# Reordering k scalings on GpSimd, one pair of steps on TensorE at the start, and moving two last copies to VectorE in a fused linear-attention and MLP kernel

## Chip, cores, metric

One core of a Trainium2 chip. The metric is the device time of one execution in microseconds (us). In the profiles PE is TensorE, PEld its weight loads, DVE is VectorE, ACT is ScalarE, POOL is GpSimd, SP is SyncE; L170 is line 170 of the kernel. The tiles live in SBUF or, where TensorE writes, in banks of PSUM. An expert matmul is one of `x @ w_in` of the MLP (`h_ps`).

## The reference, cut

```python
# q, k, v: (4, 8, 768, 64) float32; lam: one decay per head
for b in range(nb):                                   # blocks of the sequence
    intra = (qb @ kb.T) * Dmask                       # scores, masked by powers of lam
    inter = (qb * lam_pow) @ kv_state
    out[block] = intra @ vb + inter
    kv_state = lam_block * kv_state + (kb * rev_pow).T @ vb
x = out.transpose(0, 2, 1, 3).reshape(3072, 512)
y = gelu_exact(x @ w_in) @ w_out                      # 512 -> 2048 -> 512
```

## The kernel before

It works on 24 chunks of 128 tokens (4 batches, 6 steps), and on the MLP in 6 groups of 4 chunks. The program gives every engine its order, and GpSimd's timeline of before shows it kept: q_hat of chunk 9 at 53.29, the four k_dec from 54.29, the next load issue at 58.27, as in the code below. Chunks 0 to 7 are transposed on TensorE, the others by DMA, after GpSimd has scaled q. The parts that matter here, cut:

```python
def decay_k(c, eng):                     # k times powers of lam, both operands in SBUF
    c.k_dec = work_pool.tile([128, H, D], BF16, tag="kd", name="k_dec", bufs=8)
    eng.tensor_mul(c.k_dec, c.k, lam_m[...])

def scores(c):                           # takes two PSUM banks of tag "sc" (4 banks in turn)
    sc_ps = [bank([128, HP, C], F32, "sc", f"sc_ps{hi}") for hi in range(2)]
    ...
    # VectorE: sc_m = sc_ps * dmask

def next_state(c):                       # one bank of the same tag "sc"
    kv_ps = bank([128, HP, 128], F32, "sc", "kv_ps")
    ...                                  # TensorE: kv_ps = k_dec.T @ v
    nc.vector.tensor_add(tmp, kv_ps, states[c.b])   # the sum: empties the bank
    nc.vector.tensor_mul(new, tmp, lam_blk)         # the product: both inputs in SBUF

def first_requests():                    # on GpSimd, all in this order
    for n in (8, 9):
        request(n)                       # q_hat = q * lam_p, then DMA transposes
    for n in range(4, 8):
        decay_k(live[n], nc.gpsimd)
    prefetch(11)                         # six load issues for chunks 10 and 11
    for n in (8, 9):
        decay_k(live[n], nc.gpsimd)
# on TensorE: kv(4, 5) before block (1, 6), kv(6, 7) before (1, 8), scores of 8 and 9 before (1, 12)
```

(2 * M is written as 8 here, and so on.) The four states of chunks 4 to 7 take the four "sc" banks just before the scores of chunks 8 and 9 take them again: the second bank of chunk 9's scores is the bank that the state of chunk 7 used.

## Time and profile before

| | before |
|---|---|
| median of the first 3 runs | 212.79 us (212.71 to 213.16) |
| span of the profile | 211.0 us |
| PE busy | 97% of the span |
| PE's wait for k_dec in this profile | 0.24 us |

TensorE is busy all through, so only its few waits count, and what follows its last matmul. The lines that show this are in the prediction. One more line of the timeline of VectorE before will be needed: the state products (L219), of which the first began 20 ns after GpSimd had begun a k_dec (57.29).

```profile
57.31 1.57 DVE L219 TENSOR_TENSOR state<-tmp,lam_blk 128x512 bf16<-128x512 f32 x1
59.52 0.69 DVE L219 TENSOR_TENSOR state<-tmp,lam_blk 128x512 bf16<-128x512 f32 x1
60.84 0.89 DVE L219 TENSOR_TENSOR state<-tmp,lam_blk 128x512 bf16<-128x512 f32 x1
62.37 0.81 DVE L219 TENSOR_TENSOR state<-tmp,lam_blk 128x512 bf16<-128x512 f32 x1
```

The columns are start, duration, engine, line, operation, tiles, shapes, number of instructions merged into the line; in brackets the idle time before it and what ended it.

### The profile page before, as it was taken

Reading aid. Unit: us, or ns where it says so; the run is one execution under the profiler, and the core shown is the slowest. Engines: PE = TensorE matmul, PEld = TensorE weight load, DVE = VectorE, ACT = ScalarE, POOL = GpSimd, SP = SyncE. Lnnn points to the kernel's source line nnn. Section 1 sums busy time; section 2 is a strip of 40 time slices with the busy share of each in tenths; the row PEclk is TensorE's granted clock in tenths of the full one; section 3 lists DMA queues with packets and bytes.
Section 4 is the critical chain, followed back from the end, with each engine's and each line's share of the span. In section 5 each row is a group of like instructions: output and inputs, shape, how many; then the busy total and the mean of one; then the engine's idle time right before and its main releaser. Section 6 shows DMA issues by size and latency. Waiting matters only on the chain.

```text
span 211.0 us, 3635 instructions
## 1 busy us (share of the span) xinstructions
PE 205.7 (97%) x1503; PEld 107.2 (51%) x1503; DVE 78.1 (37%) x124; ACT 86.6 (41%) x153; POOL 104.3 (49%) x119
## 2 busy tenths in 40 slices
PE   7999999999999999999999999999999999999994
PEld 2455574556664465444465444555444464444442
DVE  4783610175594136840414842244542240000000
ACT  5675662326556111556111556311465311566121
POOL 7994633883898964948978695940000000000000
PEclk9999999999999999999999999999999999999999
DMA  7999999999899699996999999996100012100112
GB/s 85 141 152 183 196 207 194 155 212 159 172 96 129 77 138 111 116 134 160 136 156 141 159 172 140 132 170 164 50 0 3 0 50 102 50 0 0 50 53 99
DMA packets 101328, 24.49 MB, mean 116 GB/s; under 512 B 92992, under 2 KB 98368, under 8 KB 101312
## 3 DMA queue, kind: packets, MB, share of 16 engines
q0 software_dynamic: 79120, 13.51, 84.3%
q1 hardware_dynamic: 22192, 10.76, 25.1%
q8 instruction: 12, 0.20, 0.4%
q14 instruction: 4, 0.03, 0.0%
HBM read 27.27 MB, written 6.29 MB: 159 GB/s over the span
## 4 chain that ended last, share of the span: by engine, by line
PE 71%; DMA 19%; POOL 8%; issue 1%; ACT 0%; POOLq 0%
PE o_ps L277 31%; PE h_ps L265 31%; DMA w_out_t<-in_moe_w_out_dram 7%; DMA w_in_t<-in_moe_w_in_dram 4%; DMA v_t<-in_v_dram 4%; DMA q_t<-in_q_dram 3%; PE sc_ps L199 2%; PE o_ps L232 2%; POOL k_dec L170 2%; PE o_ps L226 2%; PE o_ps L291 2%; POOL q_t L66 2%; PE kv_ps L211 1%; POOL k_t L66 1%; POOL v_t L66 1%
## 5 line engine op out<-in xcount | busy, mean ns | idle before, releaser
L265 PE MATMUL h_ps<-x_t,w_in_t 128*128 128x512 bf16 (+2 forms) x464 | 86.6, 343 | 0.1
L277 PE MATMUL o_ps<-w_out_t,g_t 128*128 128x512 bf16 x368 | 82.9, 379 | 0.0
L267 ACT ACTIVATE g_t<-h_ps 128x512 bf16<-128x512 f32 (+1 forms) x101 | 58.2, 576 | 33.9 <-PE h_ps L265 33.7
L265 PEld LDWEIGHTS <-w_in_t 128*128 128x128 bf16 x464 | 41.0, 98 | 39.9 <-DMA w_in_t<-in_moe_w_in_dram 0.2
L277 PEld LDWEIGHTS <-g_t 128*128 128x128 bf16 x368 | 35.0, 98 | 40.8
L203 DVE TENSOR_TENSOR sc_m<-sc_ps,dmask 128x512 bf16<-128x512 f32 x48 | 30.0, 682 | 39.2 <-PE sc_ps L199 39.2
L282 ACT COPY o_sb<-o_ps 128x512 f32<-128x512 f32 x23 | 13.5, 586 | 73.5 <-PE o_ps L277 73.5
L191 POOL TENSOR_TENSOR q_hat<-q_t,lam_p 128x512 bf16<-128x512 bf16 x16 | 17.0, 1065 | 23.2 <-DMA q_t<-in_q_dram 14.0
L66 POOL DMA_DIRECT2D q_t<-in_q_dram x24 | 21.6, 902 | 5.0 <-DMA w_out_t<-in_moe_w_out_dram 3.3
L66 POOL DMA_DIRECT2D k_t<-in_k_dram x24 | 22.1, 920 | 3.2 <-DMA w_out_t<-in_moe_w_out_dram 1.1
L66 POOL DMA_DIRECT2D v_t<-in_v_dram x23 | 20.9, 911 | 2.9 <-DMA w_out_t<-in_moe_w_out_dram 2.3
L238 DVE CAST x_t<-o_ps 128x512 bf16<-128x512 f32 x18 | 11.3, 684 | 19.8 <-PE o_ps L232 19.8
L170 POOL TENSOR_TENSOR k_dec<-k_t,lam_m 128x512 bf16<-128x512 bf16 x16 | 17.2, 1104 | 0.0
L218 DVE TENSOR_TENSOR tmp<-kv_ps,state 128x512 f32<-128x512 f32 x16 | 10.9, 683 | 10.1 <-PE kv_ps L211 10.1
L219 DVE TENSOR_TENSOR state<-tmp,lam_blk 128x512 bf16<-128x512 f32 x16 | 12.8, 803 | 0.5
L326 PE MATMUL idle_ps<-idle 128*128 128x512 bf16 x31 | 10.9, 477 | 1.2 <-DVE idle L106 1.2
L184 DVE TENSOR_TENSOR qT<-t_ps,lam_q 128x512 bf16<-128x512 bf16 x8 | 5.5, 688 | 14.1 <-PE t_ps L178 13.3
L199 PE MATMUL sc_ps<-qT,kT 64*128 64x128 bf16 x192 | 8.0, 217 | 0.9 <-DVE qT L184 0.6
L199 PEld LDWEIGHTS <-kT 64*128 64x128 bf16 x192 | 5.7, 94 | 5.8 <-issue 4.3
L232 PE MATMUL o_ps<-sc_m,v_t 128*64 128x128 bf16 x192 | 7.8, 222 | 0.0
L183 ACT COPY kT<-t_ps 128x512 bf16<-128x512 bf16 x8 | 4.7, 586 | 6.0 <-PE t_ps L178 5.8
L232 PEld LDWEIGHTS <-v_t 128*64 128x64 bf16 x192 | 5.8, 109 | 2.6 <-issue 0.7
(41 smaller groups left out, 71.9 us busy)
## 6 DMA issues: line engine op xcount, KB each, us to landing
out_dram<-o_sb SPq DMA_DIRECT2D x23, 256.0 KB, 2.4
k_t<-in_k_dram POOLq DMA_DIRECT2D x24, 128.0 KB, 4.9
q_t<-in_q_dram POOLq DMA_DIRECT2D x24, 128.0 KB, 5.4
v_t<-in_v_dram POOLq DMA_DIRECT2D x23, 128.0 KB, 5.9
w_out_t<-in_moe_w_out_dram POOLq DMA_DIRECT2D x4, 512.0 KB, 13.3
w_in_t<-in_moe_w_in_dram POOLq DMA_DIRECT2D x4, 384.0 KB, 9.8
w_in_t<-in_moe_w_in_dram POOLq DMA_DIRECT2D x2, 256.0 KB, 7.6
v_f<-in_v_dram SPq DMA_DIRECT2D x1, 256.0 KB, 3.5
```

What stands on the lines that cost most here:

```text
L66: nc.gpsimd.dma_start(raw[n, name], chunk_of(name, n))
L170: eng.tensor_mul(c.k_dec, c.k, lam_m[:, :, None].to_broadcast((128, H, D)))
L191: nc.gpsimd.tensor_mul(q_hat, c.q, lam_p[:, :, None].to_broadcast((128, H, D)))
L199: nc.tensor.matmul(sc_ps[hi][:, hp, :], c.kT[p, hp, :], c.qT[p, hp, :], start=True, stop=True)
L203: nc.vector.tensor_mul(c.sc_m[:, :, hi, :], sc_ps[hi], dmask_r[:, :, hi, :])
L219: nc.vector.tensor_mul(new, tmp, lam_blk)
L232: nc.tensor.matmul(c.o_ps[hi * D:(hi + 1) * D, hp, :], c.v[:, 2 * hp + hi, :], c.sc_m[:, hp, hi, :], start=(c.so == 0 and hp == 0), stop=T ...
L238: nc.vector.tensor_copy(x_o, c.o_ps)
L265: nc.tensor.matmul(h_ps[:, f, :], w, x_t[:, ki, lo:hi], start=(ki == 0 and f == 0), stop=(ki == NK1 - 1), skip_group_check=True)
L267: nc.scalar.activation(g_t[:, kf:kf + n_kf, lo:hi], h_ps, ACT.Gelu)
L277: nc.tensor.matmul(om[io], g_t[:, kf, io * C:(io + 1) * C], w_out_t[:, kf, :], start=(kf == 0), stop=(kf == NK2 - 1))
L282: nc.scalar.copy(o_sb, om[io])
```

## The change

The intent, part by part: GpSimd does the k_dec of chunks 4 to 7 while it would otherwise wait for q, so that the states don't wait; the scores of chunk 2 don't stand behind the outputs of chunk 1; the last rows leave PSUM through VectorE.

```diff
@@ mm2_cols
-                nc.scalar.copy(o_sb, o2)
+                nc.vector.tensor_copy(o_sb, o2)
@@ start
-    keep_warm(2)
+    keep_warm(4)
+    scores(live[2])
     outputs(live[1])
-    scores(live[2])
-    keep_warm(5)
+    keep_warm(4)
     outputs(live[2])
@@ first_requests
         for n in (2 * M, 2 * M + 1):
+            for m in (2 * n - 3 * M, 2 * n - 3 * M + 1):
+                decay_k(live[m], nc.gpsimd)
             request(n)
-        for n in range(M, 2 * M):
-            decay_k(live[n], nc.gpsimd)
         prefetch(2 * M + 3)
```

## The prediction

Where a cut is marked, figures and rules of the hardware are taken out that no trace or run shows. The sum keeps its terms, 0.24 + 0.05 + 0 = 0.29 us less and 0.05 back, 212.55; but what the end's 0 was worked out from, the cost of a copy on VectorE, is cut, so this 0 was the author's estimate and is not shown. Three things to know for reading: the 265 and 478 ns on ScalarE are the copies of 128 and 384 columns; the 0.85 for four idle matmuls is an estimate (in the profile of before the four from 14.98 start 0.215 to 0.227 us apart, and take 0.87 up to the next matmul); and that VectorE stands up to 1.0 us (rival A) is an estimate from the 1.57 us of the one product beside a k_dec and the 1.04 us of a k_dec.

> **What bounds the kernel now.** I read the page first (busy shares, the slices), then the waits, then the chain that ended last, and then the timelines of single engines around the three places that the diff touches: the start (11 to 16 us), the stretch where chunks 4 to 7 enter the state (48 to 63 us), and the end. The page says that TensorE is the bound nearly everywhere:
>
> ```profile
> PE 205.7 (97%) x1503; PEld 107.2 (51%) x1503; DVE 78.1 (37%) x124; ACT 86.6 (41%) x153; POOL 104.3 (49%) x119
> PE   7999999999999999999999999999999999999994
> PEclk9999999999999999999999999999999999999999
> ```
>
> PE is at nine tenths or more in 38 of 40 slices and the clock is granted throughout. Only what makes PE wait, or what follows its last matmul, can be won. The waits of the whole execution that hold up PE after the start are one line, and it belongs to the group that the diff moves (the weight loads of the state update waiting for GpSimd's scaled k):
>
> ```profile
> PE sc_ps L199 <- DVE qT L184: 0.6, 2, 0.4
> PEld L232 <- DMA v_t<-in_v_dram: 0.5, 1, 0.5
> PEld L211 <- POOL k_dec L170: 0.2, 1, 0.2
> ```
>
> The chain shows the same place: GpSimd, queued since the start behind its DMA issues and two scalings of q, releases the state matmuls at 58.39, and from there to the end everything is PE:
>
> ```profile
> 53.29 1.04 POOL q_hat L191
> 54.33 1.63 POOL k_dec L170 x2
> ...
> 56.29 2.05 POOL k_dec L170 x2
> 58.34 0.05 issue
> 58.39 0.40 PE kv_ps L211 x4
> ```
>
> GpSimd's 8% and the DMA's 19% in that chain are therefore not a prize of 27%: PE had other work meanwhile. The prize is PE's own stop. In PE's timeline the four state updates of that stretch come in two pairs:
>
> ```profile
> 56.16 0.62 PE L211 MATMUL kv_ps<-v_t,k_dec 128*128 128x128 bf16 x8
> 57.92 0.86 PE L211 MATMUL kv_ps<-v_t,k_dec 128*128 128x128 bf16 x8
> ```
>
> Same work, 0.62 against 0.86: the second pair stops 0.24 us in its middle, for k of chunk 7.
>
> [...] the product of tmp and lam_blk (both in SBUF) took 1.57 us at 57.31, beside GpSimd's k_dec, and 0.69 us at 59.52 beside DMA issues. The score masks and casts take one operand from PSUM and stay at 0.68 to 0.69. [...] The trace has ScalarE at 265 ns and 478 ns, and VectorE at 680 ns for 512 elements[...]. [...] The trace has a PE gap of 0.42 us at 8.16 with the clock at 1.00 afterwards[...].
>
> **The change, part by part.**
>
> **GpSimd's order.** Removed from behind q_hat 9: four k_dec (54.29 to 58.27, 3.98 us, 0.995 each from start to start). Added: k 4 and 5 ahead of q_hat 8, k 6 and 7 between q_hat 8 and q_hat 9. GpSimd's timeline has idle time just there:
>
> ```profile
> 47.24 0.88 POOL L66 DMA_DIRECT2D v_t<-in_v_dram  x1
> 50.91 1.04 POOL L191 TENSOR_TENSOR q_hat<-q_t,lam_p 128x512 bf16<-128x512 bf16 x1 [2.79 <-DMA q_t<-in_q_dram]
> 53.29 1.04 POOL L191 TENSOR_TENSOR q_hat<-q_t,lam_p 128x512 bf16<-128x512 bf16 x1 [1.34 <-DMA q_t<-in_q_dram]
> 54.29 4.04 POOL L170 TENSOR_TENSOR k_dec<-k_t,lam_m 128x512 bf16<-128x512 bf16 x4
> 58.27 0.94 POOL L66 DMA_DIRECT2D k_t<-in_k_dram  x1
> ```
>
> The gaps are 2.79 and 1.34 us. k of chunks 4 to 7 is on the chip (chunk 7's transpose runs at 49.2 on PE). So: k 4, 5 from 48.1 to 50.1, inside the gap of 2.79; q_hat 8 stays at 50.9; k 6, 7 from 51.9 to 53.9; q_hat 9 from 53.9 to 54.9, that is 0.6 later than 53.29; the next loads from 54.9 in place of 58.27, 3.3 us earlier (3.98 less 0.6). All four k_dec are done 2.2 us ahead of PE's 56.16, where before the last two ended at 57.3 and 58.3. PE's stop of 0.24 us goes, and nothing else on PE does: after 60 us its timeline has no wait left. The 3.3 us that GpSimd gains later are off the path.
>
> **The start.** One more idle matmul in all (4+4 for 2+5[...]) and the scores of chunk 2 ahead of the outputs of chunk 1. PE now:
>
> ```profile
> 11.55 0.59 PE L326 MATMUL idle_ps<-idle 128*128 128x512 bf16 x2
> 12.11 0.58 PE L232 MATMUL o_ps<-sc_m,v_t 128*64 128x128 bf16 x8
> 12.90 0.40 PE L199 MATMUL sc_ps<-qT,kT 64*128 64x128 bf16 x8 [0.21 <-DVE qT L184]
> 13.23 1.25 PE L326 MATMUL idle_ps<-idle 128*128 128x512 bf16 x5
> 14.42 0.63 PE L232 MATMUL o_ps<-sc_m,v_t 128*64 128x128 bf16 x8
> 14.98 1.04 PE L326 MATMUL idle_ps<-idle 128*128 128x512 bf16 x4
> 15.85 1.46 PE L265 MATMUL h_ps<-x_t,w_in_t 128*128 128x384 bf16 x8
> ```
>
> The scores of chunk 2 already wait for VectorE's qT, which runs 12.17 to 12.85 straight behind the masks of chunk 1. VectorE's order is not touched, so they start at 12.90 in either kernel. With the change four idle matmuls end at 11.55 + 0.85 = 12.40, PE waits half a microsecond, the scores run to 13.23, the outputs of chunk 1 take about 0.35, four idle matmuls 0.85 and a switch 0.1: outputs of chunk 2 from 14.53 in place of 14.42. But their second matmul needs the second mask, which VectorE ends at 14.61. It starts at 14.66 before, and can do so after. The last four idle matmuls and the first expert matmul at 15.85 stay. Sum: 0. A small gain is possible in executions where v of chunk 1 lands later than here (the wait of 0.5 above), because it then no longer holds the scores; I put 0.05 on it.
>
> **The end.** The last two evacuations move from ScalarE to VectorE. The one of 384 columns (0.48 us[...]) lies beside the last 16 matmuls. The one of 128 is on the path:
>
> ```profile
> 207.00 0.48 ACT L295 COPY o_sb<-o_ps 128x384 f32<-128x384 f32 x1 [1.97 <-PE o_ps L291]
> 207.50 1.01 SPq L296 DMA_DIRECT2D out_dram<-o_sb  x2
> 207.89 0.27 ACT L295 COPY o_sb<-o_ps 128x128 f32<-128x128 f32 x1 [0.42 <-PE o_ps L291]
> ```
>
> [...] VectorE starts perhaps 20 ns sooner after a matmul (13.32 after one that ends at 13.31; ScalarE 207.89 after 207.85). [...]
>
> **Sum**: 0.24 (state) + 0.05 (start) + 0 (end) = 0.29 us less, and 0.05 back for the risk in rival A, so 212.79 - 0.24 = 212.55.
>
> **The rivals.** A: a VectorE wait in place of the GpSimd wait. GpSimd now reaches k_dec of chunks 8 and 9 at 54.9 + 5.3 (six issues, 58.27 to 63.57) = 60.2. VectorE then does the state products of chunks 6 and 7, whose inputs are both in SBUF. By today's durations (0.72 and 0.61 from start to start) the product of chunk 6 starts at 59.97. If k_dec comes first, VectorE stands up to 1.0 us, the sum of chunk 7 ends near 62.5 in place of 62.33, and the scores of chunk 9, which take over that PSUM bank at about 62.0, wait 0.3 us: the gain is gone, 212.8. For it: the 1.57 us above. Against it: the first product is relieved of just that 0.9, so that VectorE is ahead by it, and 59.97 is before 60.2. One in four. B: q_hat 9 is 0.6 us later, and the loads of chunks 10 and 11 now run beside its DMA transposition, whose landing takes 2.4 to 6.0 us in this trace. Even at 6.0 it lands near 61.0, and its scores come at 62.0: 1 us in hand. If it doesn't hold, some tenths are lost: 212.9. One in fifteen. C: the whole GpSimd lead is worth more, because later loads and transpositions come 3.3 us earlier. Against it: no wait of PE after 60 us. It would take the time below 212.2; one in fifteen. D: the start is set by PE's order, not by VectorE's, and the extra idle matmul costs its 0.2, or the earlier scores win as much. Either moves the time by 0.2; one in six.
>
> **Range and chances.** The three runs before spread from 212.71 to 213.16, which is as much as the effect. Centre 212.55, with 0.4 down (C, or both small gains) and 0.4 up (A or B with a run at the upper edge): 212.15 to 212.95. 2% is 4.26 us, and the sum of PE's waits after the start is 0.24, so a change of 2% would take something that no view shows: 0.01 for either side, 0.98 for within.
>
> **What would show it.** In the changed kernel: no PE wait on k_dec, and both pairs of state matmuls at 0.62; GpSimd's loads after q_hat 9 near 54.9; scores of chunk 2 still near 12.9 from the span's start, ended by VectorE's qT, and the first expert matmul near 15.85; 16 score matmuls near 62.0 without a wait (with one: rival A, and a state product of over 1 us on VectorE before it)[...]. I am wrong if the first expert matmul moves by over 0.15 us, if the last copy takes over 0.35, or if a new wait shows at the scores of chunks 8 and 9.

## The result

Changed: 212.75 us median of 6 runs (212.16 to 213.04); before: 212.78 us median of 6 (212.56 to 213.16). The ratio is 0.9994, 95% interval 0.9979 to 1.001. The time is the same, though the wait that was to go is gone. PE's timeline of the changed kernel:

```profile
55.93 0.61 PE L211 MATMUL kv_ps<-v_t,k_dec 128*128 128x128 bf16 x8
...
57.68 0.61 PE L211 MATMUL kv_ps<-v_t,k_dec 128*128 128x128 bf16 x8
58.12 3.68 PE L265 MATMUL h_ps<-x_t,w_in_t 128*128 128x128 bf16 x39
61.73 0.97 PE L199 MATMUL sc_ps<-qT,kT 64*128 64x128 bf16 x16
62.64 3.63 PE L265 MATMUL h_ps<-x_t,w_in_t 128*128 128x512 bf16 x16
```

(This trace lacks some matmul records, 1480 on PE against 1504 weight loads, so counts such as x39 are one short.) Both pairs of state matmuls now take 0.61 us, where the second took 0.86. But the 16 score matmuls take 0.97 where they took 0.62. Before:

```profile
62.23 0.62 PE L199 MATMUL sc_ps<-qT,kT 64*128 64x128 bf16 x16
```

From the first state matmul to the first expert matmul behind the scores, which I call the stretch, it is 6.71 us (55.93 to 62.64) against 6.62 before (56.16 to 62.79; 6.63 from these rounded times). The chain of what ended last, changed kernel, shows who is in between (columns: start, duration, what):

```profile
57.08 1.10 DVE state L219
58.17 0.61 DVE tmp L218
58.79 0.02 issue
58.81 0.81 DVE state L219
59.62 0.61 DVE tmp L218
60.24 0.02 issue
60.26 1.41 DVE state L219
61.67 0.61 DVE tmp L218
62.28 0.04 issue
62.33 0.38 PE sc_ps L199 x7
```

In the chain of before, GpSimd's k_dec stood at this place and the scores ran through. Now VectorE's sums and products do: the sum of chunk 7 (61.67) ends at 62.28, and 0.05 later TensorE goes on with the last seven of chunk 9's eight score matmuls, the first of which writes the bank that that sum has emptied. GpSimd's timeline, changed kernel:

```profile
48.09 2.05 POOL L170 TENSOR_TENSOR k_dec<-k_t,lam_m 128x512 bf16<-128x512 bf16 x2
50.74 1.04 POOL L191 TENSOR_TENSOR q_hat<-q_t,lam_p 128x512 bf16<-128x512 bf16 x1 [0.60 <-ACT x_t L236]
51.74 2.04 POOL L170 TENSOR_TENSOR k_dec<-k_t,lam_m 128x512 bf16<-128x512 bf16 x2
53.74 1.04 POOL L191 TENSOR_TENSOR q_hat<-q_t,lam_p 128x512 bf16<-128x512 bf16 x1
54.72 0.94 POOL L66 DMA_DIRECT2D k_t<-in_k_dram  x1
...
60.01 2.55 POOL L170 TENSOR_TENSOR k_dec<-k_t,lam_m 128x512 bf16<-128x512 bf16 x2
```

The k_dec of chunks 8 and 9 stand at 60.01 in place of 63.57. The product of chunk 6 starts at 60.26, 0.25 us after the first of them, and takes 1.41 us in place of 0.69. That is the prediction's rival A. The products at 57.08 and 58.81, beside GpSimd's load issues, lost time too (1.10 and 0.81 us).

At the start, 15.54 for the first expert matmul against 15.85 looks like a gain, but everything from the first score matmul on (7.86 against 8.16) is as much earlier, and 7.69 us lie between the two in both. At the end, the last copy of the changed kernel:

```profile
207.74 0.29 DVE L295 COPY o_sb<-o_ps 128x128 f32<-128x128 f32 x1 [0.34 <-PE o_ps L291]
```

From the last matmul's end to the end of the span it is 3.18 us against 3.14 before.

### The profile page after: what moved, and what is told of

Read it like the earlier page. It is cut to its first block, busy times and chain, and to the rows that moved or that the text cites. A ratio compares the mean times of both kernels' runs of the same rounds, so it can differ in the third digit from the quotient of the medians.

```text
span 210.9 us, 3613 instructions
## 1 busy us (share of the span) xinstructions
PE 203.0 (96%) x1480; PEld 106.7 (51%) x1504; DVE 79.1 (38%) x126; ACT 86.0 (41%) x151; POOL 105.0 (50%) x119
## 4 chain that ended last, share of the span: by engine, by line
PE 86%; POOL 4%; DMA 4%; DVE 4%; issue 1%; ACT 0%; POOLq 0%
PE o_ps L277 37%; PE h_ps L265 37%; DMA w_in_t<-in_moe_w_in_dram 4%; PE sc_ps L199 3%; PE o_ps L232 3%; PE o_ps L226 2%; PE o_ps L291 2%; PE kv_ps L211 2%; DVE state L219 2%; POOL k_t L66 1%; POOL q_t L66 1%; DVE tmp L218 1%; PE t_ps L178 1%; POOL v_t L66 1%; DVE sc_m L203 0%
## 5 line engine op out<-in xcount | busy, mean ns | idle before, releaser
L277 PE MATMUL o_ps<-w_out_t,g_t 128*128 128x512 bf16 x355 | 81.4, 379 | 1.1 <-issue 0.6
L170 POOL TENSOR_TENSOR k_dec<-k_t,lam_m 128x512 bf16<-128x512 bf16 x16 | 17.7, 1134 | 0.0
L295 DVE COPY o_sb<-o_ps 128x384 f32<-128x384 f32 (+1 forms) x2 | 0.8, 424 | 34.9 <-PE o_ps L291 34.9
L326 PE MATMUL idle_ps<-idle 128*128 128x512 bf16 x31 | 9.9, 448 | 1.2 <-DVE idle L106 1.2
```

Source lines behind the costliest of these rows:

```text
L170: eng.tensor_mul(c.k_dec, c.k, lam_m[:, :, None].to_broadcast((128, H, D)))
L277: nc.tensor.matmul(om[io], g_t[:, kf, io * C:(io + 1) * C], w_out_t[:, kf, :], start=(kf == 0), stop=(kf == NK2 - 1))
```

## The experiments

Runs of one kernel on one chip scatter by 0.2 to 0.5 us (standard deviation; 0.7 for one kernel), which is as large as what is at issue. So I read each profile in three pieces: the first state matmul's time; the stretch; and last matmul to end. From the end of the stretch to the end of the last matmul it is 145.07 us in every profile (145.067 to 145.068 in 14 profiles). "Held" is what the first three state products took over 0.69 us each, in sum; "scores lost" is by how much the time from the first to the last score matmul's start exceeds 0.405 us. A dash stands where PE itself waited for k_dec, so that the scores came later anyway.

| kernel | first state matmul | held | scores lost | stretch | last matmul to end |
|---|---|---|---|---|---|
| before | 56.16 | - | 0 | 6.62 | 3.14 |
| start only | 56.10 | - | 0 | 7.24 | 3.13 |
| end only | 55.68 | - | 0 | 7.20 | 3.17 |
| changed | 55.93 | 1.25 | 0.35 | 6.71 | 3.18 |
| changed, second | 55.93 | 1.35 | 0.45 | 6.81 | 3.15 |
| changed, third | 56.21 | 1.33 | 0.44 | 6.79 | 3.15 |
| GpSimd order only | 56.08 | 1.38 | 0.49 | 6.84 | 3.12 |
| k of 8 and 9 in halves | 56.31 | 1.33 | 0.43 | 6.79 | 3.17 |
| twice as long a read | 55.60 | 1.95 | 1.05 | 7.41 | 3.17 |
| a write in its place | 56.03 | 0 | 0 | 6.36 | 3.17 |
| k of 8 and 9 before the loads | 56.12 | 0 | 0 | 6.36 | 3.17 |
| sums first | 56.61 | other order | 0 | 6.36 | 3.16 |
| candidate | 56.14 | other order | 0 | 6.36 | 3.12 |
| candidate, second | 55.96 | other order | 0 | 6.36 | 3.15 |

Theory 1: the wait for k_dec is gone, but VectorE's products are held by GpSimd, so that the bank of chunk 7's state comes free too late. Theory 2: the gain is real, and the start or the end gave it back; or the scores wait for something else.

### GpSimd order only

The first_requests hunk of the diff alone, on the kernel before.

> Only the part on GpSimd's order. Measure: the stretch from the first state matmul of chunk 4 to the first expert matmul behind the scores of chunks 8 and 9, which is 6.63 us before (56.16 to 62.79) and 6.71 us after the whole change (55.93 to 62.64). Theory 1 (the wait on k_dec is gone but a GpSimd product of chunk 8 holds up a VectorE state product, so that the scores of chunk 9 wait for their PSUM bank): both pairs of state matmuls at 0.61 to 0.62 us, one state product of over 1.3 us that starts near 60, scores at 0.9 to 1.0 us in place of 0.62, stretch 6.6 to 6.8, time within 0.2 us of before. Theory 2 (the gain on PE is real and another part of the change, start or end, gave it back): stretch 6.35 to 6.45, time 0.2 to 0.3 us below before.

212.89 us median (6 runs), before 213.34 on that chip (11 runs); ratio 0.9976 (0.9958 to 0.9994). Theory 1's profile came out: state matmuls 0.61 and 0.61, a product of 1.41, and PE's timeline names the releaser:

```profile
61.88 0.45 PE L199 MATMUL sc_ps<-qT,kT 64*128 64x128 bf16 x9
62.60 0.38 PE L199 MATMUL sc_ps<-qT,kT 64*128 64x128 bf16 x7 [0.28 <-DVE tmp L218]
```

The stretch of 6.84 is a little over the 6.6 to 6.8 expected, and the time differs from before by more than the 0.2 expected. The next two runs suggest why: with the GpSimd order of before the wait can be longer than in the first profile of before. Before itself was not profiled on that chip, so this is not shown.

### Start only, end only

The start hunk alone, and the mm2_cols hunk alone.

> Only the new order at the start. Measure: first score matmul to first expert matmul, 7.69 us before (8.16 to 15.85) and 7.68 after the whole change (7.86 to 15.54). Theory 1: 7.65 to 7.72 and the k_dec wait still there (second pair of state matmuls 0.85 us, stretch 6.6 to 6.65), time within 0.2 us of before. Theory 2, if the start is the part that gave the gain back: 7.85 or more, time 0.15 to 0.3 us above before.

> Only the last two copies on VectorE. Theory 1: last copy 0.28 to 0.30 us against 0.265 on ScalarE, from its start to the end of the span within 0.05 us of before (3.10 us), time within 0.15 us of before. Theory 2, if the end is the part that gave the gain back: 0.2 to 0.3 us longer from the last matmul to the end of the span, and as much in the time.

Start only: 213.40 us median, ratio 1.0007 (0.9987 to 1.0026). First score matmul to first expert matmul 7.80 us, between the two theories' numbers; but the three profiles with the old start have 7.69, 7.88 and 7.70, and the other profiles with the new start 7.69 to 7.87, so this is scatter and the start costs and gains nothing that can be seen. End only: 213.37, ratio 1.0006 (0.9988 to 1.0025); the last copy took 0.29.

Both keep the GpSimd order of before, and in both PE's wait for k_dec is larger than the 0.24 us that the prediction read off. PE and VectorE of the start-only kernel:

```profile
58.03 0.39 PE L211 MATMUL kv_ps<-v_t,k_dec 128*128 128x128 bf16 x4
58.95 0.40 PE L211 MATMUL kv_ps<-v_t,k_dec 128*128 128x128 bf16 x4 [0.53 <-POOL k_dec L170]
```

```profile
57.26 0.74 DVE L219 TENSOR_TENSOR state<-tmp,lam_blk 128x512 bf16<-128x512 f32 x1
```

and its GpSimd:

```profile
54.40 4.49 POOL L170 TENSOR_TENSOR k_dec<-k_t,lam_m 128x512 bf16<-128x512 bf16 x4
```

In the first profile of before GpSimd's last k_dec began at 57.29 and VectorE's product at 57.31, and the product took 1.57 while the four k_dec took 4.04. Here the product came first (57.26, the k_dec 57.40) and took 0.74, and the four k_dec took 4.49, the last of them 1.49. In both profiles the one that began second took longer, 1.57 us in place of 0.69 or 1.49 in place of 1.04, and PE waited longer where that was GpSimd (0.53 us in the line above, 0.24 in the first profile of before). (GpSimd's last k_dec also began 0.07 to 0.17 us later after the first state matmul in these two profiles than in that of before.) So the stretch is 6.62 to 7.24 us with the order of before (three profiles), and 6.71 to 6.84 with the changed order (four). Whether the change is worth anything in time depends on which of the two engines came first before.

### Sums first

The changed kernel, with both sums of a pair of states ahead of both products on VectorE (beside a k_dec a product took 1.57 us in before and 1.41 in the changed kernel; a sum took 0.68 beside the second k_dec of the changed kernel):

```diff
-            nc.vector.tensor_mul(new, tmp, lam_blk)
+            products.append(lambda: nc.vector.tensor_mul(new, tmp, lam_blk))
@@ kv
-        for n in ns:
-            next_state(live[n])
-            take_state(live[n])
+        for i in range(0, len(ns), 2):
+            for n in ns[i:i + 2]:
+                next_state(live[n])
+                take_state(live[n])
+            while products:
+                products.pop(0)()
```

> The whole change, and VectorE does both sums of a pair of state updates (which empty the PSUM banks) ahead of both products (which contend with GpSimd). No instruction more or less. Theory 1: the scores of chunk 9 no longer wait, even if a product is still held for up to 1 us: scores at 0.62 us, stretch 6.35 to 6.45 (6.63 before, 6.71 after), time 0.2 to 0.35 us below the changed kernel and 0.2 to 0.3 below before. Theory 2 (the scores wait for something else, as the landing of the transposed q of chunk 9, which is 0.2 us later than before): scores still at 0.9 us or more, stretch 6.6 to 6.8, no change in time.

212.24 us median against 213.34 before; ratio 0.9958 (0.9942 to 0.9974). VectorE and PE:

```profile
60.33 1.28 DVE L220 TENSOR_TENSOR tmp<-kv_ps,state 128x512 f32<-128x512 f32 x2
61.53 3.38 DVE L221 TENSOR_TENSOR state<-tmp,lam_blk 128x512 bf16<-128x512 f32 x2
```

```profile
62.42 0.62 PE L199 MATMUL sc_ps<-qT,kT 64*128 64x128 bf16 x16
```

The time fell by 1.10 us between the medians, far more than the 0.2 to 0.3 expected, and more than the stretch explains (0.26 to 0.88 us against the three profiles with the order of before); where the rest comes from is not shown, and the profile is of the slowest of the six runs (212.96). In the profile the products are still held (3.38 us for two), but they now come behind the sums that free the banks, and the scores run through: 6.36. So it is the bank, freed by the sum, and nothing else that the scores waited for; the late q of chunk 9 is out. This run also shows how the start gives things back: its first expert matmul came at 15.22, the earliest of all, and its first state matmul at 56.61, the latest, because the weights had not landed:

```profile
PEld L267 <- DMA w_in_t<-in_moe_w_in_dram: 1.6, 3, 0.8
```

(the waits view: us in total, times, longest). Before had 0.2 us of this wait.

### k of chunks 8 and 9 before the loads

```diff
-        prefetch(2 * M + 3)
         for n in (2 * M, 2 * M + 1):
             decay_k(live[n], nc.gpsimd)
+        prefetch(2 * M + 3)
```

> The whole change, and GpSimd scales k of chunks 8 and 9 ahead of the six load issues of chunks 10 and 11, not behind them[...]. Theory 1 (the hold of a VectorE state product by a GpSimd product causes the wait of the scores): no state product over 1.2 us, scores at 0.62 us, stretch from the first state matmul of chunk 4 to the first expert matmul behind the scores 6.35 to 6.45 us (6.71 changed, 6.36 with the sums first), time 0.2 to 0.5 us below the changed kernel of the same chip. Theory 2 (it is the loads that run beside, or the landing of q of chunk 9): scores still 0.9 us or more, stretch 6.6 or more.

The profile is as theory 1 says: GpSimd's k_dec end at 57.0, all four products take 0.69 us (the first is shown), the scores 0.62, the stretch 6.36.

```profile
57.27 0.69 DVE L219 TENSOR_TENSOR state<-tmp,lam_blk 128x512 bf16<-128x512 f32 x1
```

```profile
61.93 0.62 PE L199 MATMUL sc_ps<-qT,kT 64*128 64x128 bf16 x16
```

The time was 212.72 us median, ratio to before 0.9973 (0.9948 to 0.9999), and the changed kernel in the same call had 212.63: the expected 0.2 to 0.5 us did not show in six runs.

### k of chunks 8 and 9 in halves

```diff
+            for h in (slice(0, HP), slice(HP, H)):
+                nc.gpsimd.tensor_mul(c.k_dec[:, h], c.k[:, h], lam_m[:, h, None].to_broadcast((128, HP, D)))
```

in place of decay_k for chunks 8 and 9, on the changed kernel.

> The dose halved: the whole change, with each scaling of k of chunks 8 and 9 in two instructions of half the size. Theory 1: an instruction of GpSimd is about 0.55 us, so the state product of chunk 6 is held at most so long and takes 0.7 to 1.2 us in place of 1.41; the scores wait 0 to 0.1 us in place of 0.3; stretch 6.35 to 6.5. Theory 2: unchanged, 6.7 or more.

(The 0.55 us is an estimate, about half of the 1.04 us of a whole k_dec; the four halves took 3.29 us in all.) A miss: the stretch stayed at 6.79. VectorE shows why.

```profile
57.46 1.18 DVE L219 TENSOR_TENSOR state<-tmp,lam_blk 128x512 bf16<-128x512 f32 x1
59.27 1.12 DVE L219 TENSOR_TENSOR state<-tmp,lam_blk 128x512 bf16<-128x512 f32 x1
61.02 1.11 DVE L219 TENSOR_TENSOR state<-tmp,lam_blk 128x512 bf16<-128x512 f32 x1
```

The third product, beside the halves, lost 0.42 in place of 0.72, as it should. But the second lost 0.43 (0.12 in the changed kernel), beside load issues, and the sum of all three is again 1.33. It is the sum that counts: in every run of the table in which the scores lost time, they lost the sum less 0.90 us. So theory 1 was half of it. The scores have 0.90 us in hand; the k_dec alone takes 0.72, the first two products, beside load issues, lose 0.53 to 0.66 in the four profiles with whole k_dec, and only both together are too much.

### A read twice as long, and a write, at the same place

Both on the version with k of chunks 8 and 9 before the loads. Between the loads of chunk 10 and those of chunk 11 GpSimd does one spare instruction:

```diff
+        prefetch(2 * M + 2)
+        nc.gpsimd.tensor_mul(filler[:, :H, :], dmask, dmask)     # the read; for the write:
+        nc.gpsimd.memset(filler, 0.0)                            # 128x2048 fp32
         prefetch(2 * M + 3)
```

> One look. As in the kernel with k of chunks 8 and 9 ahead of the loads, and between the loads of chunks 10 and 11 GpSimd fills a spare tile of 128x2048 fp32 with zeros: busy, but reading nothing of SBUF, from about 59.4[...] over the state product of chunk 6 (59.9). If it is GpSimd's reading that holds a VectorE product with two SBUF inputs: products at 0.69 to 0.8 us, scores at 0.62 us, stretch 6.35 to 6.40. If any GpSimd work beside it holds the product: one product of 1.5 us or more, scores longer, stretch above 6.45.

> One look. The same place, but GpSimd multiplies a 128x1024 fp32 tile with itself into the spare tile (an estimated 2 us, twice the elements of a k_dec): it reads SBUF. Theory 1: one product of VectorE held up to 2 us. In the four runs with a wait of the scores so far, the time the scores lost was the sum of what the first three products lost over 0.69 us, less 0.90 us (1.25 gives 0.35, 1.35 gives 0.45, 1.38 gives 0.49, 1.33 gives 0.43): the same rule should hold here within 0.05 us, so for a hold of 1.5 us a wait of about 0.6 and a stretch of about 6.95. If the rule fails by over 0.1, the holds are not the whole cause.

The write took 1.84 us and held nothing:

```profile
59.51 1.84 POOL L390 MEMSET filler<- 128x2048 f32 x1
```

```profile
59.84 0.69 DVE L220 TENSOR_TENSOR state<-tmp,lam_blk 128x512 bf16<-128x512 f32 x1
```

The read took 2.05 us and held a product by 0.97; a product ahead of it, which began beside load issues, lost 0.97 as well:

```profile
58.08 1.66 DVE L220 TENSOR_TENSOR state<-tmp,lam_blk 128x512 bf16<-128x512 f32 x1
60.38 1.67 DVE L220 TENSOR_TENSOR state<-tmp,lam_blk 128x512 bf16<-128x512 f32 x1
```

```profile
62.70 0.38 PE L200 MATMUL sc_ps<-qT,kT 64*128 64x128 bf16 x7 [0.84 <-DVE tmp L219]
```

The sum is 1.95 us, the rule gives 1.95 - 0.90 = 1.05, and the scores lost 1.05. So here a busy GpSimd alone did not hold the product (0.69 us beside the write); GpSimd's reading fits (1.67 us beside the read). (One profile each, and the write, a fill with zeros, differs from the read, a multiplication, in its operation too.)

### The candidate, and the changed kernel beside it

The candidate is the changed kernel with the sums first, with k of chunks 8 and 9 before the loads, and with the last copies back on ScalarE. It was run twice, and the changed kernel as it is twice more.

> The candidate to beat both: the change's GpSimd order and start, both remedies (sums before products, k of chunks 8 and 9 before the loads), and the last copies back on ScalarE, which had 3.12 us from the last matmul to the end against 3.17 on VectorE. Theory 1: stretch 6.35 to 6.40, last matmul to end 3.12 to 3.14, time 0.3 to 0.6 us below the changed kernel and 0.5 to 1.1 below before on the same chip. If the remedies undo each other or the copies give nothing: the time of the kernel with the sums first, within 0.1 us.

> The changed kernel once more, as it is, for a comparison on the same chip. Theory 1: stretch 6.7 to 6.85 with one state product over 1.3 us; last matmul to end 3.15 to 3.18; time 0 to 0.5 us below before, depending on how long before waits for k_dec on this chip.

> The candidate once more (sums first, k of chunks 8 and 9 early, last copies on ScalarE), beside the changed kernel on one chip, because single runs scatter by 0.3 to 0.4 us and the first comparison (212.66 against 212.63) did not show the 0.45 us that the stretch gained in the profiles. If the profiled gain is a gain of time: 0.3 to 0.5 us below the changed kernel in the mean of the fast runs. If the start's waits for loads absorb it: the same time within 0.15 us.

> The changed kernel, for the comparison with the candidate on one chip: stretch 6.7 to 6.85 with a product of 1.41 us; time 0.1 to 0.6 us below before; 0.3 to 0.5 above the candidate if the profiled gain is one of time.

| | before | changed | candidate |
|---|---|---|---|
| first | 213.29 (11 runs) | 212.63, ratio 0.9973 (0.9951 to 0.9995) | 212.66, ratio 0.998 (0.9951 to 1.0009) |
| second | 212.80 (11 runs) | 212.71, ratio 0.9993 (0.9976 to 1.001) | 212.36, ratio 0.9976 (0.9957 to 0.9995) |

(Medians in us; ratios to before.) In all four profiles the pieces are as expected: 6.81 and 6.79 us for the changed kernel, 6.36 twice for the candidate. In time the second shows 0.35 us between the medians, the first none, with one candidate run of 214.17 in it. Over both the medians of 12 runs each are 212.70 and 212.56. The stretch is shorter by 0.44 to 0.45 us in the profiles; that as much arrives in the time is not shown, only that it is not in contradiction. The candidate is below before in both; the interval excludes equality in the second only. The sums-first version did best against before (0.9958), but was not run beside the candidate.

## Why the prediction came out as it did

212.75 lies in the range, 0.2 above the centre. That alone says little, for the range (212.15 to 212.95) holds the time of before, 212.78, as well: the net gain of 0.24 us on which the centre stood did not come. Of the prediction's three signs of being wrong two came, the new wait at the scores and a first expert matmul that moved by 0.31 us; the latter is the start's scatter, since everything from the first score matmul on moved with it. By its own steps:

- **GpSimd's order: right.** k 4 to 7 fit into the two gaps, q_hat 9 began at 53.74 (predicted 53.9), the loads at 54.72 (54.9), and PE's wait of 0.24 us went.
- **What that wait is worth: mis-sized for before.** The 0.24 us is one execution. In the two other profiles with that order the stretch is 7.20 and 7.24 in place of 6.62, mainly because VectorE came first and GpSimd last. The prediction used the 1.57 us product as evidence for rival A, but didn't see that the same meeting, won by the other side, sets the wait.
- **Rival A: the step that failed is its chance.** I gave it one in four; it came in all four profiles with the changed GpSimd order, VectorE's order as before, and k of chunks 8 and 9 whole behind the loads, with a wait of 0.35 to 0.49 us (0.3 predicted) and the time that it named (212.8). The argument against it was that the first product is "relieved of just that 0.9". It was relieved of 0.88 beside k_dec and lost 0.41 again beside load issues, and the second lost 0.12. The prediction's times, moved by the 0.23 us by which this profile is earlier, are 59.74 for the product of chunk 6 and 59.97 for GpSimd's k_dec. The k_dec came at 60.01, the product at 60.26: 0.52 late, which is these two losses, so VectorE came second. I had taken 0.69 for a product beside load issues from the one at 59.52, though the two after it in the same timeline, also beside issues, took 0.89 and 0.81.
- **The start: right**, as a sum of 0. The 0.05 for late v can't be seen in the scatter. PE's stop before the scores of chunk 2 was 0.33 us, and the clock granted from 12 to 13 us was 1.00.
- **The end: mis-sized.** The copy of 128 columns took 0.29 us on VectorE against 0.27 on ScalarE before (that of 384 columns 0.56 against 0.48), and VectorE started no sooner: 0.04 us after the last matmul on either engine. From the last matmul to the end the nine profiles with VectorE have 3.145 to 3.175 us, mean 3.165, the five with ScalarE 3.121 to 3.148, mean 3.131. So the end costs 0.03 us, where the sum had 0.
- **Rivals B, C, D: none came.** With the sums first the scores ran through, so q of chunk 9 was there; after the stretch all profiles are alike, so the GpSimd lead buys nothing later.

In the two first profiles: first state matmul 0.23 earlier (start scatter), stretch 0.09 longer, end 0.04 longer, together 0.11 us less, as the spans have it (210.99 and 210.88). The change turned a wait for GpSimd's result into a wait for a VectorE product that took 1.41 us beside GpSimd's k_dec, in place of 0.69.

## What to carry to other kernels

When an engine is moved earlier, list what it will now run beside, and for GpSimd look for VectorE instructions with two SBUF inputs there (here a product took 1.41 us beside a k_dec in place of 0.69, while a sum, with one input in PSUM, stayed at 0.68); one short instance in a profile is no measure for the others. Put the instruction that frees a PSUM bank ahead of the one that can be held up (here the stretch went from 6.71 to 6.36 us). And compare pieces of profiles when the scatter of whole runs (here 0.2 to 0.5 us) is as large as the effect.

## What the runs show of the hold, and what stays open

- A product of VectorE, with two SBUF inputs, and a k_dec of GpSimd: 1.57 us for a product that came second and 1.49 us for a k_dec that came second (0.69 and 1.04 alone); 0.69 us for a product beside a fill of 1.84 us.
- The same product beside GpSimd's load issues took from 0.69 up to 1.23 us, and once 1.66 (58.08 to 59.74, the last 0.30 of it beside the spare read). What in an issue holds it, and why all four products took 0.69 beside the same kind of issues in the runs with k of chunks 8 and 9 early and no spare read, stays open.
- The last copy, 128 columns from PSUM, took 0.29 us on VectorE and 0.27 on ScalarE; this is most of the 0.03 us that the end lost.
- In a timeline the held time is part of the instruction's duration (1.41 us for 0.69), and the wait view shows no wait of VectorE there.
